# Sinkhorn-sorted attention and a mixture of experts: seven products for all four experts of the middle chunk, PSUM banks that stay in their pools, and loads in another order

## The chip, the cores and the metric

The kernel runs on one core of a Trainium2 chip. The metric is the device time of one execution in microseconds (us). Each kernel is executed several times and the median is given. The core has five engines that run beside one another: TensorE multiplies matrices, VectorE (DVE in the profile) and ScalarE (ACT) work on tiles in on-chip memory and evacuate the results of matmuls from PSUM, GpSimd (POOL) does some elementwise work and issues loads, and SyncE (SP) issues most other transfers. PSUM, where TensorE writes, has eight banks of 512 fp32 numbers per partition, and this kernel uses all of them.

## The reference, cut to what matters

```python
P = sort_net                                  # (4, 8, 8, 8)
for _ in range(5):                            # rows and columns normalised
    P = np.exp(P - P.max(-1)); P /= P.sum(-1); P /= P.sum(-2)
k_sorted = einsum('bhij,bhjcd->bhicd', P, k_blocks)    # blocks of 96 tokens mixed
v_sorted = einsum('bhij,bhjcd->bhicd', P, v_blocks)
attn = softmax(q_block @ k_sorted_block.T / 8)         # within each block
x = (attn @ v_sorted_block)  ->  (3072, 512)           # 4 batches x 768 tokens, 8 heads x 64
p = domain_probs / domain_probs.sum(-1)
out = sum over 4 experts e of  p[:, e] * (relu(x @ w1[e]) @ w2[e])   # 512 -> 1024 -> 512
```

Attention takes a small part of the matmul work, the four experts nearly all of it.

## The kernel before: the parts that the change touches

The tokens of each batch are worked through in three chunks of 256. A chunk has a first layer (x times w1, relu, times p, result in Hb) and a second layer (Hb times w2, result stored). While the experts of one batch are computed, the attention of a later batch is computed beside them: a plan names, for each slot between groups of matmuls, which stage is to run there. `st_v` mixes values, `st_k` keys, `st_q` transposes queries by DMA, `st_s` makes scores, `st_a` multiplies with the values, and `st_x` transposes the result into xT.

```python
PLANS = { ...                                           # (chunk, slot, stage, batch, part)
    1: [ ...
        (1, 3, st_k, 3, 1), (1, 4, st_v, 3, 2), (1, 4, st_q, 3, 3), (1, 4, st_bk, 3, 1), (1, 5, st_s, 3, 1),
        (1, 6, st_k, 3, 2), (1, 7, st_k, 3, 3), (1, 8, st_v, 3, 3), (1, 9, st_a, 3, 0), (1, 10, st_s, 3, 2),
        (1, 11, st_a, 3, 1), (1, 11, st_x, 3, 0), (1, 12, st_s, 3, 3), (1, 13, st_a, 3, 2), (1, 13, st_x, 3, 1),
        (1, 14, st_a, 3, 3), (2, 0, st_x, 3, 2), (2, 1, st_x, 3, 3),
    ], }
```

From the third chunk of batch 1 on (g = G0 = 5 of 12), a block of the first layer is computed after Winograd's scheme: instead of eight products of half-size blocks there are seven, and sums of the weights (s1, s3, n2, s4) and of the tokens (t1, n2, t3, t4) are formed beforehand. `seven` holds the seven products of one expert. X, Z and Q are PSUM banks; X must be a copy of Z at one point, and ScalarE makes it.

```python
def seven(g, e):
    ...
    def product(dst, lhs, rhs, first=False):            # eight matmuls of 128 columns
    ...
    def p1(): product(Z, "a11", "b11", True); nc.scalar.copy(X, Z)
    def p5(): product(Q, "s1", "t1", True)
    def p6(): product(X, "n2", "n2"); nc.scalar.copy(u2, X)
    def p2(): product(Z, "a12", "b21"); finish(0, 0, Z)
    def p7(): product(X, "s3", "t3"); nc.scalar.copy(u3, X); tt(t22, Q, u3, ALU.add)
    def p4(): product(X, "a22", "t4"); finish(1, 0, X)
    def p3(): product(Q, "s4", "b22"); tt(t12, Q, u2, ALU.add)
```

Before that chunk the banks belong to two pools, psM and psA, of two tiles of two banks each. At the chunk they are closed one after the other and given anew. The chunk's expert 0 is still computed directly (`chunk_first`), as banks of psM are free before those of psA:

```python
def last_banks(n):
    (openA, openM)[n].close()
    pool = ctx.enter_context(tc.tile_pool(name=f"ps7_{n}", bufs=1, space=PSUM, ...))
    ...
    nc.tensor.matmul(last["X"][n][:], w1sb[0][:, 0, 0:P], w1sb[0][:, 1, 0:512], start=True, stop=True)   # marks X as written

def last_chunk(g, slot=None):
    ...
    if lead:                                            # g == G0
        chunk_first(b, c, [0], 0, slot)                 # expert 0: 2 groups of 16 matmuls of 256 columns
        last_banks(0)
        last_tmp(g)
        prs = {1: seven(g, 1)}
        prs[1][1](); prs[1][5](); seven(g, 2)[5](); prs[1][2](); prs[1][6]()
        input_sums(0, 0, True); input_sums(0, 1, True)
        last_banks(1)
    else: ...                                           # later chunks: expert 0 was begun in the chunk before
    ...
    product(bankQ, sm(0), "t1");         nc.scalar.copy(p5[:], bankQ)
    product(bankA, sm(1), "t2", False);  nc.scalar.copy(u2[:], bankA)
    ...
    product(bankQ, blk(1, 0), "b22", False, range(2))   # experts 0 and 1
    ...
    product(bankA, blk(0, 1), "t3", False)
    ...
    tt(ob2, bankA, p5[:], ALU.add); tt(ob1, bankA, ob1, ALU.add)
    nc.sync.dma_start(o[:, 2 * c + 1, :], ob[:])
    ...
    product(bankQ, blk(1, 0), "b22", False, range(2, E), ...)   # experts 2 and 3
    tt(oa2, bankQ, u2[:], ALU.add)
    if final:
        nc.sync.dma_start(o[:, 2 * c, DH:Dm], oa2)
```

While the experts work on batch 0, GpSimd issues the loads of batch 1, all in one queue behind those of the experts' weights:

```python
for qd in range(2):
    for nm in ("v", "k"):
        load_natural(1, nm, qd)          # values, keys: four heads each
    if qd == 0:
        load_queries(1, range(2))        # queries of heads 0 and 1, in pieces of 64 numbers
```

Of the kernel before, what the change touches and what calls it, by code (L numbers as in the profile page):

```python
# [17 lines left out]
def kernel(  # L18
# [38 lines left out]

    openM, openA = [ctx.enter_context(ExitStack()) for _ in range(2)]
    psM = openM.enter_context(tc.tile_pool(name="psM", bufs=2, space=bass.MemoryType.PSUM))
    psA = openA.enter_context(tc.tile_pool(name="psA", bufs=2, space=bass.MemoryType.PSUM, side="right"))  # L60
    att = ctx.enter_context(tc.tile_pool(name="att", bufs=2))
# [368 lines left out]
    def st_a(b, pr):  # L430
        if b == B - 1 and pr >= H // 2 - 2:
            xsl = Sflat[:, ds((pr + 4) * NB * 2 * D, NB * 2 * D)].rearrange("p (i h d) -> p i h d", i=NB, h=2)[0:BLK]
        else:
            xsl = att.tile([P, NB, 2, D], F16, name=f"xsl_{b}_{pr}", tag="xsl")[0:BLK]
        xsls[(b, pr)] = xsl
        vs = vss[(b, pr // 2)]
        for hh in range(2):
            ET = ETs[2 * (pr % 2) + hh]
            ps = psa([P, 2, 512], F32, f"ps_a_{b}_{pr}_{hh}")
            for i in range(NB):  # L440
                nc.tensor.matmul(  # L441
                    ps[:, i // HB, ds((i % HB) * VW, D + 1)],
                    ET[:, ds(i * BLK, P)],
                    vs[:, i, 2 * (pr % 2) + hh, 0:D + 1],
                    start=True, stop=True,
                )
            normalize(ps, xsl, hh)
# [153 lines left out]
    def st_bk(b, qd):  # L601
# [25 lines left out]
            (1, 0, st_k, 3, 0), (1, 1, st_v, 3, 1), (1, 1, st_x, 2, 3), (1, 1, st_q, 3, 2), (1, 2, st_s, 3, 0),  # L627
            (1, 3, st_k, 3, 1), (1, 4, st_v, 3, 2), (1, 4, st_q, 3, 3), (1, 4, st_bk, 3, 1), (1, 5, st_s, 3, 1),
            (1, 6, st_k, 3, 2), (1, 7, st_k, 3, 3), (1, 8, st_v, 3, 3), (1, 9, st_a, 3, 0), (1, 10, st_s, 3, 2),
            (1, 11, st_a, 3, 1), (1, 11, st_x, 3, 0), (1, 12, st_s, 3, 3), (1, 13, st_a, 3, 2), (1, 13, st_x, 3, 1),  # L630
            (1, 14, st_a, 3, 3), (2, 0, st_x, 3, 2), (2, 1, st_x, 3, 3),
        ],
# [152 lines left out]
    def chunk(b, c, slot, done=()):  # L785
# [34 lines left out]

        if b or c:
            two = [psm([P, 2, 512], F32, f"ps_p{n}_{b}_{c}") for n in range(2)]
            bankA, bankB, bankC, bankQ = [two[n // 2][:, n % 2, 0:DH] for n in range(4)]
        if b:
            times(bankA, blk(0, 0), "b11", es)
            slot()
            times(bankB, blk(1, 0), "b21", es)
            slot()
            nc.scalar.copy(p1[:], bankA)
            tt(oa1, bankB, p1[:], ALU.add)  # L830
            times(bankQ, sm(0), "t1", es)
            nc.scalar.copy(p5[:], bankQ)
            slot()
            for e in es:
                h_sums(e, 3, True)
            times(bankA, sm(1), "t2", es, False)
            nc.scalar.copy(u2[:], bankA)
            slot()
            for e in es:
                h_sums(e, 4, True)  # L840
            times(bankC, blk(1, 1), "n4", es)
            nc.scalar.copy(ob1, bankC)
            slot()
            times(bankA, blk(0, 1), "t3", es, False)
            tt(ob2, bankA, p5[:], ALU.add)
            tt(ob1, bankA, ob1, ALU.add)
            store(1, ob)
            slot()
            times(bankQ, blk(1, 0), "b22", es, False)
            tt(oa2, bankQ, u2[:], ALU.add)  # L850
            slot()
            store(0, oa)
            return
# [94 lines left out]

    A_ORDER = (12, 13, 3, 6, 7, 8, 0, 1, 2, 9, 10, 11)
    As = []  # L950
# [41 lines left out]

    last = {}

    def last_banks(n):

        (openA, openM)[n].close()
        pool = ctx.enter_context(tc.tile_pool(name=f"ps7_{n}", bufs=1, space=bass.MemoryType.PSUM, side=("right", "left")[n]))
        for nm, m in (("X", 1), ("Z", 1), ("Q", 2)):
            last[nm] = last.get(nm, []) + [  # L1000
                pool.tile([P, 512], F32, tag=f"{nm}{i}", name=f"ps_{nm}{n}{i}") for i in range(m)
            ]

        nc.tensor.matmul(last["X"][n][:], w1sb[0][:, 0, 0:P], w1sb[0][:, 1, 0:512], start=True, stop=True)

    def last_tmp(g):

        room = []
        if g > G0:
            t = moe.tile([P, NKC, NB, BLK], F16, name="tmp7", tag="xT").rearrange("p k i x -> p (k i x)").bitcast(F32)  # L1010
            room += [t[:, ds(n * 512, 512)] for n in range(3)]
        for m in range(2):
            t = att.tile([P, NB, 4, VW], F16, name=f"tmp7_{g}_{m}", tag="vs").rearrange("p i h w -> p (i h w)")
            t = t[:, 0:2048].bitcast(F32)
            room += [t[:, 0:512], t[:, 512:1024]]
        for m in range(1 if g > G0 else 2):
            t = att.tile([P, NB, 2, D], F16, name=f"tmp7x_{g}_{m}", tag="xsl").rearrange("p i h d -> p (i h d)")
            room.append(t.bitcast(F32))
# [3 lines left out]
        else:  # L1022
            last["u2"] = last["t12"] = room[0::2]
            last["u3"] = last["t22"] = room[1::2]

    def seven(g, e):

        a, t, pb = As[e], Bs[g], pbs[divmod(g, R // 2)]
        n = e - (g == G0)
        X, Z = [last[nm][n % len(last[nm])][:] for nm in ("X", "Z")]  # L1030
        u2, u3, t22, t12 = [last[nm][n % len(last[nm])] for nm in ("u2", "u3", "t22", "t12")]
        Q = last["Q"][e if n == e else (0, 0, 1, 3)[e]][:]
        tt = nc.vector.tensor_tensor
# [21 lines left out]

        def p1():
            product(Z, "a11", "b11", True)
            nc.scalar.copy(X, Z)  # L1058

# [29 lines left out]
    def last_begin(g):  # L1089
        last["e0"] = seven(g, 0)  # L1090
        last["e0"][1]()
        last["e0"][5]()

    def last_chunk(g, slot=None):
        b, c = divmod(g, R // 2)
        final = g == GN - 1
        lead = int(g == G0)
        if lead:
            chunk_first(b, c, [0], 0, slot)
            last_banks(0)  # L1100
            last_tmp(g)
            prs = {1: seven(g, 1)}
            prs[1][1]()
            prs[1][5]()
            seven(g, 2)[5]()
            prs[1][2]()
            prs[1][6]()
            input_sums(0, 0, True)
            input_sums(0, 1, True)
            last_banks(1)  # L1110
        else:
            last["e0"][2]()
            prs = {0: last["e0"]}
        for e in range(1 + lead, E):
            prs[e] = seven(g, e)
        for e in range(1 + lead, E):
            now, prev = prs[e], prs[e - 1]
            now[1]()
            prev[7]()
            if e > 1 + lead:  # L1120
                prs[e - 2][12]()
            if not lead or e > 2:
                now[5]()
            now[2]()
# [10 lines left out]

        def product(ps, lhs, rhs, first=True, es=range(E), between=None, at=E - 1):
            for e in es:
                if e == at and between:
                    between()
                for f in range(KH):  # L1140
                    nc.tensor.matmul(  # L1141
                        ps, lhs(e, f), Ts[e][rhs][:, f, :],
                        start=(first and e == 0 and f == 0), stop=(e == E - 1 and f == KH - 1), skip_group_check=True,
# [26 lines left out]
        for e in range(E):  # L1170
            h_sums(e, 4, True)
        if lead:
            for e in range(E):
                h_sums(e, 3, True)
            input_sums(0, 2, True)
        product(bankQ, sm(0), "t1")
        nc.scalar.copy(p5[:], bankQ)
        product(bankA, sm(1), "t2", False)
        nc.scalar.copy(u2[:], bankA)
        if not lead:  # L1180
            for e in range(E):
                h_sums(e, 3, True)
        product(bankQ, blk(1, 0), "b22", False, range(2))
        if not final:
# [8 lines left out]
        nc.sync.dma_start(o[:, 2 * c + 1, :], ob[:])  # L1193
        if lead:
            input_sums(0, 3, True)
        product(bankQ, blk(1, 0), "b22", False, range(2, E), None if final else last["e0"][6], 3)
        tt(oa2, bankQ, u2[:], ALU.add)
        if final:
            nc.sync.dma_start(o[:, 2 * c, DH:Dm], oa2)
        else:  # L1200
            nc.sync.dma_start(o[:, 2 * c, :], oa[:])


    PLAN_A = [
        (1, 8, 1, 0, True), (1, 8, 1, 1, True), (1, 8, 1, 2, True), (1, 10, 1, 3, True),
        (1, 8, 2, 0), (1, 8, 2, 1), (1, 9, 3, 0), (1, 10, 3, 1), (1, 11, 2, 2), (1, 12, 3, 2), (1, 13, 2, 3),
        (2, 0, 3, 3),
    ]
# [94 lines left out]
    h_q(0, 1, vec)  # L1303
    second_layer0(0, next_stages)
    for qd in range(2):
        for nm in ("v", "k"):
            load_natural(1, nm, qd)
        if qd == 0:
            load_queries(1, range(2))
    chunk_first(0, 0, [1, 2], 1, next_stages)  # L1310
# [64 lines left out]
```

The softmax here doesn't subtract the row's maximum and nothing guards it: scores larger than these inputs give would overflow.

## Time and profile before

| | before |
|---|---|
| time, median of three executions | 363.17 us (362.46 to 363.51) |
| span in the profile | 362.4 us, granted TensorE clock 1.00 throughout |
| VectorE, ScalarE, GpSimd busy | 276.8, 173.6, 134.1 us |
| DMA queues, share of 16 engines | 41.6% GpSimd's queue, 27.4% SyncE's |
| HBM read, written | 42.00 MB, 6.34 MB |

A line of the waits names who waited, for whom, and gives microseconds in total, the number of waits and the longest. A line of the chain gives the start, the length and the engine with its tile. A line in order of time gives the start, the length, the engine, the line of the kernel, the operation, the tiles and the number of instructions merged in it; in square brackets stands the idle time ahead of it and what ended it. Starts are exact; the ends of matmuls are modelled and include the way through the array.

### The profile page before, as it was taken

The page shows a single profiled execution, that of the slowest core. Times are in us where ns is not written, and L with a number is a line of the kernel's source. Part 1 is how long each engine was busy: PE and PEld are TensorE (multiplying, and loading weights), DVE is VectorE, ACT ScalarE, POOL GpSimd, SP SyncE. Part 2 cuts the span into 40 slices and gives each one's busy share as a digit, 9 for nine tenths or more (in the row PEclk, how much of TensorE's full clock was granted, in tenths as well). Part 3 has the DMA queues.
Part 4 walks back from the last instruction along what each step waited for, and adds up shares of the span by engine and source line. Part 5 has one row for each costly group of instructions (what it writes and reads, how often), then busy time and mean ns, then how long its engine had stood idle before and what let it go on. Part 6 is the DMA issues. An engine that isn't in the chain of part 4 may idle for free.

```text
span 362.4 us, 10776 instructions
## 1 busy us (share of the span) xinstructions
PE 354.0 (98%) x4589; PEld 315.0 (87%) x4589; DVE 276.8 (76%) x560; ACT 173.6 (48%) x305; POOL 134.1 (37%) x148
## 2 busy tenths in 40 slices
PE   8899999989999999999999999999999999999996
PEld 8785857778888888988889999999999998999995
DVE  5654898769788777868978978867779679587794
ACT  2664330451434355377938257165283481561740
POOL 8872010736022330000626318137055082180470
PEclk9999999999999999999999999999999999999999
DMA  7999999999999999935995210210401201102101
GB/s 99 207 207 231 209 209 202 194 187 194 214 116 142 203 127 173 165 70 69 179 192 88 60 60 2 60 60 3 89 32 50 70 3 58 62 2 63 56 15 46
DMA packets 71676, 40.47 MB, mean 112 GB/s; under 512 B 40518, under 2 KB 66380, under 8 KB 71628
## 3 DMA queue, kind: packets, MB, share of 16 engines
q0 software_dynamic: 36560, 19.93, 41.6%
q1 hardware_dynamic: 35068, 19.85, 27.4%
q8 instruction: 36, 0.59, 0.7%
q14 instruction: 12, 0.10, 0.1%
HBM read 42.00 MB, written 6.34 MB: 133 GB/s over the span
## 4 chain that ended last, share of the span: by engine, by line
PE 75%; DMA 18%; DVE 3%; SPq 1%; ACT 1%; issue 1%; POOL 0%; DVEq 0%; ACTq 0%; POOLq 0%
PE ps_Q L1141 24%; PE ps_h L768 13%; PE ps_p L753 10%; PE ps_X L1038 10%; DMA arena<-in_q_dram 8%; PE ps_Q L1038 7%; PE ps_Z L1038 7%; DMA w<-in_moe_w_dram 6%; DMA vs<-arena 2%; DMA qT<-arena 2%; PE ps_a L441 2%; PE ps_s L406 1%; SPq L368 1%; PE ps_v L354 1%; PE ps_k L387 1%
## 5 line engine op out<-in xcount | busy, mean ns | idle before, releaser
L1051 POOL TENSOR_TENSOR Hb<-tmp,pb 128x512 f16<-128x512 f32 x40 | 50.8, 1277 | 84.3 <-ACT tmp L1050 83.1
L768 PE MATMUL ps_h<-xT,w 128*128 128x256 f16 x576 | 67.8, 273 | 0.0
L768 PEld LDWEIGHTS <-w 128*128 128x128 f16 x576 | 55.1, 98 | 7.4
L774 DVE SCALAR_TENSOR_TENSOR Hb<-ps_h,pb 128x1024 f16<-128x1024 f32 x36 | 44.0, 1223 | 19.8 <-PE ps_h L768 19.6
L1141 PEld LDWEIGHTS <-Hb 128*128 128x128 f16 x560 | 53.4, 98 | 5.6
L1038 PEld LDWEIGHTS <-w 128*128 128x128 f16 x864 | 52.4, 98 | 1.0
L1141 PE MATMUL ps_Q<-w,Hb 128*128 128x256 f16 x336 | 43.4, 273 | 0.0
L1038 PEld LDWEIGHTS <-arena 128*128 128x128 f16 x552 | 33.4, 98 | 0.3 <-issue 0.2
L413 ACT ACTIVATE ET<-ps_s 96x768 f16<-96x768 f32 x24 | 18.1, 802 | 28.4 <-PE ps_s L406 28.1
L121 POOL DMA_DIRECT2D arena<-in_q_dram x24 | 19.9, 836 | 26.9 <-DMA qT<-arena 16.6
L1038 PE MATMUL ps_X<-kT,arena 128*128 128x128 f16 x384 | 29.3, 219 | 0.1
L1074 DVE TENSOR_TENSOR tmp<-ps_Q,tmp 128x512 f32<-128x512 f32 x26 | 18.0, 692 | 14.6 <-ACT tmp L1073 10.4
L1058 ACT COPY ps_X<-ps_Z 128x512 f32<-128x512 f32 x27 | 15.4, 570 | 28.3 <-PE ps_Z L1038 27.9
L396 ACT CAST kT<-ps_k 64x384 f16<-64x384 f32 x48 | 22.7, 473 | 12.8 <-PE ps_k L387 11.8
L739 DVE TENSOR_TENSOR Sb<-Hb 128x512 f16<-128x512 f16 x45 | 26.3, 609 | 0.9 <-POOL Hb L1051 0.8
L1141 PE MATMUL ps_Q<-T,Hb 128*128 128x256 f16 x224 | 26.7, 273 | 0.0
L1050 ACT ACTIVATE tmp<-tmp 128x512 f32<-128x512 f32 x40 | 25.4, 634 | 1.2 <-DVE tmp L1074 1.0
L753 PEld LDWEIGHTS <-Hb 128*128 128x128 f16 x232 | 21.9, 98 | 3.0
L1141 PEld LDWEIGHTS <-Sb 128*128 128x128 f16 x224 | 21.9, 98 | 2.5
L1065 ACT COPY tmp<-ps_X 128x512 f32<-128x512 f32 x26 | 15.2, 586 | 13.2 <-PE ps_X L1038 13.2
L1051 POOL TENSOR_TENSOR Hb<-tmp7x,pb 128x512 f16<-128x512 f32 x14 | 19.0, 1356 | 5.7 <-ACT tmp7x L1050 5.7
L1044 DVE SCALAR_TENSOR_TENSOR Hb<-ps_X,pb 128x512 f16<-128x512 f32 x27 | 18.5, 684 | 2.7 <-PE ps_X L1038 2.7
(205 smaller groups left out, 652.7 us busy)
## 6 DMA issues: line engine op xcount, KB each, us to landing
w<-in_moe_w_dram POOLq DMA_DIRECT2D x7, 1024.0 KB, 27.4
pb<-p_dram SPq DMA_DIRECT2D x12, 512.0 KB, 5.4
arena<-in_k_dram POOLq DMA_DIRECT2D x8, 384.0 KB, 8.8
arena<-in_v_dram POOLq DMA_DIRECT2D x8, 384.0 KB, 8.9
vs<-arena SPq DMA_DIRECT2D x36, 66.0 KB, 5.7
arena<-in_q_dram POOLq DMA_DIRECT2D x24, 96.0 KB, 7.3
out_dram<-ob SPq DMA_DIRECT2D x9, 256.0 KB, 2.0
out_dram<-oa SPq DMA_DIRECT2D x8, 256.0 KB, 2.3
```

Source lines behind the costliest of these rows:

```text
L121: nc.gpsimd.dma_start(t[:, h // 2, :, h % 2, :], q[b, h].rearrange("(t p) d -> p t d", p=P))
L396: nc.scalar.copy(kT[ds(D * hh, D), r], pk[ds(D * r, D), hh].rearrange("p a (i c) -> p a i c", c=CP),)
L413: nc.scalar.activation(ETs[2 * (pr % 2) + hh][:, 0:S].rearrange("c (a x) -> c a x", a=2), pss[hh][0:BLK, :, 0:HS], AF.Exp, bias=0.0, scale ...
L739: tt(sm[0], blk(0, 1), blk(1, 1), ALU.add)
L753: nc.tensor.matmul(ps, lhs(e, f), Ts[e][rhs][:, f, :], start=(first and e == es[0] and f == 0), stop=(done and e == es[-1] and f == KH - 1 ...
L768: nc.tensor.matmul(ps[:, f, :], w1sb[e][:, kc, ds((4 * g + f) * P, P)], xT[:, kc, ds(2 * c * P, 2 * P)], start=(kc == 0), stop=(kc == NKC ...
L774: nc.vector.scalar_tensor_tensor(out=Hb[:, e, ds(4 * g, 4), :], in0=ps[:], scalar=0.0, op0=ALU.max, in1=pb[:, ds(e, 1), :].broadcast_to([P ...
L1038: nc.tensor.matmul(dst[:, ds(f * P, P)], a[lhs][:, k, ds(f * P, P)], t[rhs][:, k, :], start=(first and f == 0 and k == 0), stop=(f == KH - ...
L1044: nc.vector.scalar_tensor_tensor(out=Hb[:, e, ds(i * KH, KH), ds(j * P, P)], in0=src.rearrange("p (f x) -> p f x", f=KH), scalar=0.0, op0= ...
L1050: nc.scalar.activation(src, src, AF.Relu, bias=0.0, scale=1.0)
L1051: nc.gpsimd.tensor_tensor(Hb[:, e, ds(i * KH, KH), ds(j * P, P)], src.rearrange("p (f x) -> p f x", f=KH), pb[:, ds(e, 1), ds(j * P, P)].b ...
L1141: nc.tensor.matmul(ps, lhs(e, f), Ts[e][rhs][:, f, :], start=(first and e == 0 and f == 0), stop=(e == E - 1 and f == KH - 1), skip_group_ ...
```

## The change: what it does and what it is for

1. The third chunk of batch 1 computes expert 0 by seven products too. It is begun in the chunk before, within that chunk's last product, as the later chunks do it for one another.
2. For this the eight banks stay in the two pools for the whole kernel. The chunk before takes X, Z and two Q banks from psM as ordinary tiles and uses them for its own sums as well; the third chunk takes the other four from psA.
3. The input sums of expert 0 (s1, s3, n2, s4) are formed earlier, on VectorE, in slots of the second chunk; their place in memory moves (A_ORDER), and so does that of two attention tiles (xsl), which now lie where the values of batch 3 lay. So these values must be used up sooner: `st_v(3, 3)` moves from slot 8 to slot 4.
4. The queries of heads 0 and 1 of batch 1 are loaded ahead of the values and keys.
5. At the very end the last column half of the output is computed and stored in two pieces of 128 columns, in two banks and through two queues.

```diff
-    openM, openA = [ctx.enter_context(ExitStack()) for _ in range(2)]
-    psM = openM.enter_context(tc.tile_pool(name="psM", bufs=2, space=bass.MemoryType.PSUM))
-    psA = openA.enter_context(tc.tile_pool(name="psA", bufs=2, space=bass.MemoryType.PSUM, side="right"))
+    psM = ctx.enter_context(tc.tile_pool(name="psM", bufs=2, space=bass.MemoryType.PSUM))
+    psA = ctx.enter_context(tc.tile_pool(name="psA", bufs=2, space=bass.MemoryType.PSUM, side="right"))
...
-            xsl = Sflat[:, ds((pr + 4) * NB * 2 * D, NB * 2 * D)]...
+            xsl = arena[:, ds((pr + 2) * NB * 2 * D, NB * 2 * D)]...
...
-            (1, 3, st_k, 3, 1), (1, 4, st_v, 3, 2), (1, 4, st_q, 3, 3), (1, 4, st_bk, 3, 1), (1, 5, st_s, 3, 1),
-            (1, 6, st_k, 3, 2), (1, 7, st_k, 3, 3), (1, 8, st_v, 3, 3), (1, 9, st_a, 3, 0), (1, 10, st_s, 3, 2),
+            (1, 3, st_k, 3, 1), (1, 4, st_q, 3, 3), (1, 4, st_v, 3, 2), (1, 4, st_v, 3, 3), (1, 4, st_bk, 3, 1), (1, 5, st_s, 3, 1),
+            (1, 6, st_k, 3, 2), (1, 7, st_k, 3, 3), (1, 9, st_a, 3, 0), (1, 10, st_s, 3, 2),
...
-            (1, 14, st_a, 3, 3), (2, 0, st_x, 3, 2), (2, 1, st_x, 3, 3),
+            (2, 0, st_x, 3, 2), (2, 1, st_x, 3, 3),
...                                   # in chunk(), the chunk before
-        if b or c:
+        if (b, c) == divmod(G0 - 1, R // 2):
+            last_banks(1)
+            bankA, bankB, bankC, bankQ = [last[nm][at][:, 0:DH] for nm, at in (("X", 1), ("Z", 1), ("Q", 2), ("Q", 3))]
+        elif b or c:
...
-            times(bankQ, blk(1, 0), "b22", es, False)
+            if last["X"]:
+                last_tmp(G0, range(1), ())
+                last_begin(G0)
+
+                def between():
+                    last["e0"][6]()
+                    st_a(B - 1, H // 2 - 1)
+
+                times(bankQ, blk(1, 0), "b22", es, False, True, between, 2)
+            else:
+                times(bankQ, blk(1, 0), "b22", es, False)
...
-    A_ORDER = (12, 13, 3, 6, 7, 8, 0, 1, 2, 9, 10, 11)
+    A_ORDER = (12, 13, 14, 6, 7, 8, 0, 1, 2, 9, 10, 11)
...
+        pair = [(psa, psm)[n]([P, 2, 512], F32, f"ps7_{n}_{m}") for m in range(2)]
+        for nm, at, m in (("X", n, 0), ("Z", n, 1), ("Q", 2 * n, 2), ("Q", 2 * n + 1, 3)):
+            last[nm][at] = pair[m // 2][:, m % 2]
...
     def last_begin(g):
-        last["e0"] = seven(g, 0)
-        last["e0"][1]()
-        last["e0"][5]()
+        last["e0"] = e0 = seven(g, 0)
+        if g == G0:
+            e0[1](lambda: (e0[5](), written(1)))      # written: the marking matmul; p1 copies Z to X after it
+        else:
+            e0[1]()
+            e0[5]()
...                                   # in last_chunk()
+        last["e0"][2]()
         if lead:
-            chunk_first(b, c, [0], 0, slot)
+            last["e0"][7]()
+            slot()
             last_banks(0)
...
+        ends = [(bankQ, ds(0, P), nc.scalar), (bankB, ds(P, P), nc.sync)] if final else [(bankQ, ds(0, DH), nc.sync)]
+        for bank, part, _ in ends:
+            product(bank[:, part], sm(0), "t1", part=part)
+            nc.scalar.copy(p5[:, part], bank[:, part])
...
+        early = 1 if final else 2
+        for bank, part, _ in ends:
+            product(bank[:, part], blk(1, 0), "b22", False, range(early), part=part)
...
+        for bank, part, queue in ends:
+            product(bank[:, part], blk(1, 0), "b22", False, range(early, E), ..., 3, part)
+            tt(oa2[:, part], bank[:, part], u2[:, part], ALU.add)
+            if final:
+                queue.dma_start(o[:, 2 * c, DH:Dm][:, part], oa2[:, part])
...
     PLAN_A = [
+        (1, 1, 0, 0, True), (1, 3, 0, 1, True), (1, 5, 0, 2, True), (2, 0, 0, 3, True),
...
-        (2, 0, 3, 3),
+        (1, 14, 3, 3),
...
+    load_queries(1, range(2))
     for qd in range(2):
         for nm in ("v", "k"):
             load_natural(1, nm, qd)
-        if qd == 0:
-            load_queries(1, range(2))
```

## The prediction

> **What bounds the kernel.** I read the page's first part, then the waits of TensorE, then the chain backwards from the longest of them, then TensorE in order of time around the chunk that is changed, then the end.
>
> ```profile
> PE 354.0 (98%) x4589; PEld 315.0 (87%) x4589; DVE 276.8 (76%) x560; ACT 173.6 (48%) x305; POOL 134.1 (37%) x148
> ...
> PE ps_s L406 <- DMA qT<-arena: 1.9, 1, 1.9
> PE ps_R L305 <- DVE sn L293: 1.1, 1, 1.1
> PE ps_w L249 <- DVE Hb L148: 1.1, 1, 1.1
> ```
>
> TensorE is busy for 354.0 of 362.4 us at full clock. Only two things can move the time: fewer or smaller matmuls, and TensorE's idle time, 8.4 us in all. Of that, 3.4 us lie behind the last matmul, some 2.2 us at the start (the two waits of 1.1), and one wait stands in the middle: 1.9 us on a transposed query tile. The chain shows where it comes from, and GpSimd in order of time shows the loads in their queue:
>
> ```profile
> 40.44 27.25 DMA arena<-in_q_dram
> 67.75 6.01 DMA qT<-arena
> 73.89 0.52 PE ps_s L406 x16
> ...
> 27.66 0.81 POOL L110 DMA_DIRECT2D arena<-in_v_dram  x1 [0.66 <-PE ps_mv L483]
> 28.46 0.75 POOL L110 DMA_DIRECT2D arena<-in_k_dram  x1
> 34.70 0.82 POOL L121 DMA_DIRECT2D arena<-in_q_dram  x1 [5.48 <-DMA w<-in_moe_w_dram]
> 40.44 0.82 POOL L121 DMA_DIRECT2D arena<-in_q_dram  x1 [4.92 <-DMA w<-in_moe_w_dram]
> ```
>
> The second query head of batch 1 was issued at 40.44 and landed at 67.7, behind the weights and the first quarters of values and keys. SyncE could have transposed from 61.5 (its load of pb was issued at 61.13) and waited until 67.75; the transpose landed at 73.8, and the scores, ready on TensorE at 72.0, began at 73.89.
>
> Then the chunk itself, TensorE in order of time:
>
> ```profile
> 181.82 1.91 PE L753 MATMUL ps_p<-w,Hb 128*128 128x256 f16 x16
> 183.56 0.94 PE L441 MATMUL ps_a<-vs,ET 96*128 96x65 f16 x16
> 184.34 3.66 PE L768 MATMUL ps_h<-xT,w 128*128 128x256 f16 x32
> 187.83 0.38 PE L1004 MATMUL ps_X<-w 128*128 128x512 f16 x1
> 188.05 0.61 PE L1038 MATMUL ps_Z<-xT,w 128*128 128x128 f16 x8
> ```
>
> Durations here include the pipe's tail; the starts are what counts. 32 matmuls of 256 columns take 187.83 - 184.34 = 3.49 us (109 ns each); a product of eight matmuls of 128 columns takes 0.447 us (starts 193.18, 193.62, 194.07), 55.9 ns each. The 16 matmuls of ps_a take 0.48 us elsewhere but 0.78 here: the second half waits for a psA tile. And the end:
>
> ```profile
> 357.93 1.04 PE L1141 MATMUL ps_Q<-w,Hb 128*128 128x256 f16 x8
> 358.97 0.33 SPq L1193 DMA_DIRECT2D out_dram<-ob  x1
> 359.07 0.42 DVE L1197 TENSOR_TENSOR oa<-ps_Q,u 128x256 f32<-128x256 f32 x1
> 359.53 0.33 SPq L1199 DMA_DIRECT2D out_dram<-oa  x1
> ```
>
> The 256 KB of ob and the 128 KB of oa are issued within 0.56 us; their packets run as one stream from 359.7 to 360.9 at 330 to 380 GB/s.
>
> [...] order of issue is order of landing (62.6, 64.6, 65.2, 67.7). [...]
>
> **The change, part by part.** *Queries first.* Nothing is added; two loads pass two others. The landings in the trace give about 2.0 us for a quarter of values or keys and 3.1 us for the pair of query heads (67.7 - 64.6; their packets are under 512 B, and run between 62 and 65 us). In the new order the pair should land near 67.7 - 4.0 = 63.7 or a little sooner, the values near 65.5, the keys near 67.7. SyncE can then issue the transpose about 4 us earlier. It stands in one ring behind pb, whose packets now run from 65.0 to 69.5; so the tile lands between 70 and 72.8, against 72.0 when TensorE wants it: I take 0.3 us as what is left of the wait. The values are wanted at 65.18 (first ps_v) and the keys at 68.45: another 0.2 us at risk. Net: 1.9 - 0.5 = 1.4 us.
>
> *Expert 0 of the third chunk by seven products.* Between the end of the t3 product (181.5) and the b11 product of the chunk (197.28) lie 15.78 us. Matmul time in it, from the starts: b22 1.75, two ps_a 0.96, the direct layer 3.49, 19 products 8.49, two marking matmuls 0.44, sum 15.13; so 0.65 us are gaps, 0.30 at the ps_a tile, the rest after the marking matmuls, where ScalarE copies Z to X with too little work beside it. After: b22 1.75, ps_a 0.96, 26 products 11.62, marks 0.44, sum 14.77: 0.36 less. Gaps: p1, p5 and the mark now lie between the two ps_a stages, so the tile is free (that stage's evacuation ended 2.5 us after t3, the second half begins at 3.2); the half of b22 (0.87 us) covers the copy of Z. From the end of t3 as zero, TensorE then stands at 0.48 (ps_a), 0.93 and 1.38 (p1, p5), 1.60 (mark), 2.47 (b22), 2.92 (p6), 3.40 (ps_a), 4.27 (b22), 4.72 and 5.17 (p2, p7), 5.39 (mark), 6.29 (p1, p5 of expert 1). ScalarE copies expert 0's u3 from 5.3 to 5.9 and expert 1's Z from 5.9 to 6.45, so p2 starts at 6.5: a wait of 0.2. p6 ends at 7.4. VectorE has two normalisations (3.3 to 5.0), an addition, a finish, t22 and s4 before the fourth token sum, which is done near 7.5: p4 waits 0.1. After that each expert takes seven products as in the later chunks, which show no wait. Gaps 0.3; gain 0.36 + 0.35 = 0.7 us.
>
> *Input sums of expert 0* move to VectorE between 156 and 166 us, 0.6 us each. Its idle stretches there are 0.85, 0.52 and 0.75 us, with two psM tiles ahead of it: no cost. *The last value stage* moves from 170.0 to about 161.9 us with its two matmuls and one cast; same work, no cost on TensorE. Banks taken from the running pools rather than from a closed one cost nothing by themselves: the same readers must be done.
>
> *The end.* 32 matmuls of 128 replace 16 of 256 twice: 32 x 55.9 against 16 x 109 is 0.04 us more each. With E the end of the last matmul's stream (358.8), before: VectorE starts at E + 0.27, takes 0.42, the last packet at E + 2.1. After: ob's addition runs 0.44 us earlier relative to E, as three experts instead of two are left; its 256 KB are gone by about E + 1.0. The last addition has 128 columns, about 0.28 us (0.69 for 512, 0.42 for 256); its 64 KB are issued at E + 0.6 and, after the 0.7 us seen between issue and packet, are gone by E + 1.5. Gain about 0.55, less 0.08: 0.5 us.
>
> Sum: 1.4 + 0.7 + 0.5 = 2.6 us off 363.17, or 360.6 us.
>
> **The rivals.** *The query wait only changes its name.* The transpose may still follow pb and the 256-byte loads of the next heads, and land near 73; or the values, now third, land late and hold the first ps_v. For it: 0.1 us of slack for the values, and pb took 8.4 us to land in this stretch. Against: before, transpose packets began only near 70, when pb was nearly through. Then 0.3 us of gain are left and the time is 361.7. *The new lead is bound by VectorE and ScalarE.* In the 15.78 us VectorE is busy for 13.05; seven products bring two more finishes and two additions (2.6 us start to start) and s4, and take away two evacuations of 1.2 and two input sums. If TensorE waits at each expert, 0.5 us are lost and the time is 361.3 to 361.8. *Everything hidden works, and the wait for queries was the only slack* that some later load needed: a load bound by the queue would show up again as a wait near 90 to 125 us; the transfers there start from TensorE's own progress, so I give it little.
>
> **Range and chances.** Head 0.3 to 1.9, lead 0.2 to 0.9, end 0.2 to 0.6; not all at one edge, and half a microsecond for the spread of the runs (362.46 to 363.51): 359.7 to 362.2. Two per cent would be 7.3 us, more than all the idle time that can be reached; losing as much would need a new wait that nothing shows. Faster by over 2%: 0.01; within: 0.98; slower: 0.01.
>
> **What would show it.** Right: no or hardly a wait of ps_s on qT; the transpose issued near 63.5; the stretch from t3 to b11 near 15.1 us; the last store's data ending 1.5 us after the last matmul. Wrong: ps_v waiting on the load of values; TensorE idle at the fourth token sum or at the copies; a new wait on a vs or xT transfer in batch 2.

## The result and the profile after

The changed kernel takes 445.97 us (445.40 to 449.34, median of six executions); beside it, on the same chip, the kernel before takes 363.03 us (362.46 to 363.51). The ratio is 1.230 (95% interval 1.226 to 1.234). Predicted were 360.6 us, with a range of 359.7 to 362.2.

The page of the changed kernel, first the busy times, then the clock that TensorE was granted in 40 slices:

```profile
PE 387.5 (87%) x4645; PEld 337.7 (75%) x4645; DVE 277.0 (62%) x563; ACT 176.8 (40%) x311; POOL 136.0 (30%) x150
...
PEclk9999999999999999989979998899698799999799
```

The other engines do what they did before (VectorE 277.0 us against 276.8), so no work has been added there. TensorE is idle for 447.6 - 387.5 = 60.1 us instead of 8.4, and its own work takes 33.5 us longer, although it has about the same number of matmuls (4645 against 4589, with more of the small ones). From slice 18 on (190 to 201 us, in the third chunk of batch 1, soon after the seven products begin) the clock is no longer always full: 0.946 in the mean of the whole span.

The waits of TensorE after (who waited, for whom: us in total, number, longest):

```profile
PE ps L1048 <- DVE Hb L1054: 24.5, 36, 1.2
PE ps L1048 <- DVE tmp L1086: 19.2, 13, 1.6
PE ps L1048 <- ACT tmp L1077: 1.8, 6, 0.3
PE ps L1147 <- DVE tmp L1086: 1.5, 1, 1.5
...
PE ps_a L440 <- DMA vs<-arena: 0.6, 1, 0.6
PE ps_s L405 <- DMA qT<-arena: 0.4, 1, 0.4
```

Before, no wait of these products is listed. Now the products (line 1048) wait 36 times for `finish` (line 1054, relu of X or Z into Hb) and 13 times for the addition that makes t22 (line 1086, reads Q). There is a second thing to read here: the tile is called `ps`, where before it was ps_X, ps_Z or ps_Q. X, Z and the two Q are no longer tiles of their own.

The second chunk of batch 2 in order of time shows which product waits for which reader. TensorE (start, length, line, operation, number; in brackets the idle time ahead and what ended it):

```profile
260.87 1.05 PE L1048 MATMUL ps<-xT,w 128*128 128x128 f16 x16 [0.29 <-ACT tmp L1077]
262.32 0.61 PE L1048 MATMUL ps<-kT,Sb 128*128 128x128 f16 x8 [0.39 <-DVE Hb L1054]
264.32 0.61 PE L1048 MATMUL ps<-kT,arena 128*128 128x128 f16 x8 [1.40 <-DVE tmp L1086]
264.77 0.61 PE L1048 MATMUL ps<-xT,w 128*128 128x128 f16 x8
266.16 0.84 PE L1048 MATMUL ps<-kT,arena 128*128 128x128 f16 x8 [0.78 <-DVE Hb L1054]
...
276.66 1.01 PE L1048 MATMUL ps<-kT,arena 128*128 128x128 f16 x8 [1.55 <-DVE tmp L1086]
277.47 1.06 PE L1048 MATMUL ps<-xT,w 128*128 128x128 f16 x8
279.31 1.01 PE L1048 MATMUL ps<-kT,arena 128*128 128x128 f16 x8 [0.78 <-DVE Hb L1054]
280.12 1.06 PE L1048 MATMUL ps<-ET,w 128*128 128x128 f16 x8
280.97 1.06 PE L1048 MATMUL ps<-xT,w 128*128 128x128 f16 x8
```

and VectorE in the same stretch:

```profile
263.58 0.69 DVE L1086 TENSOR_TENSOR tmp<-ps,tmp 128x512 f32<-128x512 f32 x1 [1.31 <-ACT tmp L1085]
265.41 0.69 DVE L1054 SCALAR_TENSOR_TENSOR Hb<-ps,pb 128x512 f16<-128x512 f32 x1 [1.14 <-PE ps L1048]
```

The product at 264.32 is p5 of expert 1. It writes that expert's Q, which nobody is reading. It starts 0.05 us after VectorE has finished the addition at 263.58 (ends at 264.27), and that addition reads the Q of expert 0: the other half of the same two-bank tile. The product at 266.16 is p6 of expert 1. It writes X of this expert, and starts 0.06 us after `finish` at 265.41 has read Z of the same pair (ends at 266.10). So TensorE, which used to work in one bank while VectorE and ScalarE emptied its neighbour, now takes turns with them. VectorE in its turn waits for ScalarE and TensorE (1.31 and 1.14 us in the brackets): each hand-over puts one engine's time behind the other's.

The last lines of the TensorE fence show the second loss. The product of eight matmuls at 280.12 is followed by the next at 280.97: 0.85 us, or 106 ns for a matmul of 128 columns, against 55.9 ns before. The granted clock of this stretch (280 to 281 us) is 0.50.

### The profile page after: what moved, and what is told of

The parts are those of the page before. It is cut to its first block, busy times and chain, and to the rows that moved or that the text cites. A ratio compares the mean times of both kernels' runs of the same rounds, so it can differ in the third digit from the quotient of the medians.

```text
span 447.6 us, 10915 instructions
## 1 busy us (share of the span) xinstructions
PE 387.5 (87%) x4645; PEld 337.7 (75%) x4645; DVE 277.0 (62%) x563; ACT 176.8 (40%) x311; POOL 136.0 (30%) x150
## 4 chain that ended last, share of the span: by engine, by line
PE 67%; DVE 13%; DMA 9%; ACT 5%; issue 3%; SPq 1%; POOL 1%; DVEq 0%; ACTq 0%; POOLq 0%
PE ps L1048 21%; PE ps L1147 17%; PE ps_h L767 12%; PE ps_p L752 6%; DVE Hb L1054 5%; DMA w<-in_moe_w_dram 3%; DVE tmp L1086 3%; DMA qT<-arena 2%; ACT tmp L1085 2%; PE ps_o L695 2%; PE ps_h L660 2%; DVE Sb L738 2%; DMA vs<-arena 2%; PE ps L752 1%; DMA room<-arena 1%
## 5 line engine op out<-in xcount | busy, mean ns | idle before, releaser
L1048 PE MATMUL ps<-kT,arena 128*128 128x128 f16 x504 | 44.7, 244 | 37.4 <-DVE tmp L1086 19.2
L1054 DVE SCALAR_TENSOR_TENSOR Hb<-ps,pb 128x512 f16<-128x512 f32 x56 | 38.6, 690 | 56.8 <-PE ps L1048 56.7
L1048 PEld LDWEIGHTS <-w 128*128 128x128 f16 x896 | 66.1, 110 | 9.1 <-issue 7.9
L767 PEld LDWEIGHTS <-w 128*128 128x128 f16 x544 | 52.0, 98 | 7.0
L1147 PE MATMUL ps<-w,Hb 128*128 128x256 f16 (+1 forms) x352 | 45.3, 274 | 2.5 <-DVE tmp L1086 1.5
L1077 ACT COPY tmp<-ps 128x512 f32<-128x512 f32 x27 | 15.8, 586 | 61.1 <-PE ps L1048 61.1
L1086 DVE TENSOR_TENSOR tmp<-ps,tmp 128x512 f32<-128x512 f32 x27 | 18.7, 691 | 30.5 <-ACT tmp L1085 29.3
L1048 PE MATMUL ps<-xT,w 128*128 128x128 f16 x384 | 33.3, 240 | 3.6 <-DVE Hb L1054 1.7
L1070 ACT COPY ps<-ps 128x512 f32<-128x512 f32 x28 | 16.0, 570 | 39.7 <-PE ps L1048 39.1
L1147 PE MATMUL ps<-T,Hb 128*128 128x256 f16 x224 | 26.7, 273 | 0.5 <-DVE oa L1168 0.5
L1048 PE MATMUL ps<-room,w 128*128 128x128 f16 x288 | 25.0, 241 | 1.9 <-DVE Hb L1054 1.0
```

The costliest lines, as they stand in the source:

```text
L767: nc.tensor.matmul(ps[:, f, :], w1sb[e][:, kc, ds((4 * g + f) * P, P)], xT[:, kc, ds(2 * c * P, 2 * P)], start=(kc == 0), stop=(kc == NKC ...
L1048: nc.tensor.matmul(dst[:, ds(f * P, P)], a[lhs][:, k, ds(f * P, P)], t[rhs][:, k, :], start=(first and f == 0 and k == 0), stop=(f == KH - ...
L1054: nc.vector.scalar_tensor_tensor(out=Hb[:, e, ds(i * KH, KH), ds(j * P, P)], in0=src.rearrange("p (f x) -> p f x", f=KH), scalar=0.0, op0= ...
L1147: nc.tensor.matmul(ps, lhs(e, f), Ts[e][rhs][:, f, part], start=(first and e == 0 and f == 0), stop=(e == E - 1 and f == KH - 1), skip_gro ...
```

## The experiments

Three theories stood after the traces. **A**: the change put X with Z, and each two Q, into one tile of two banks, and a writer waits for the readers of the whole tile. **B**: the lowered clock is the first cause, and the waits follow from slow matmuls. **C**: the new start of the third chunk and the moved sums and stages brought VectorE out of step with TensorE.

### Four banks as four tiles

Everything of the change is kept, except that X, Z and the Q are tiles of one bank. For this the running pools must again be closed one after the other.

```diff
-        pair = [(psa, psm)[n]([P, 2, 512], F32, ...) for m in range(2)]
-        last["X"][n], last["Z"][n] = pair[0][:, 0], pair[0][:, 1]        # and Q, Q from pair[1]
+        (openA, openM)[n].close()
+        pool = ctx.enter_context(tc.tile_pool(name=f"ps7_{n}", bufs=1, space=PSUM, ...))
+        last["X"][n] = pool.tile([P, 512], F32, tag="XZ0", ...)           # Z and two Q likewise
```

> The changed kernel with one thing undone: X, Z and the two Q banks of each half are four tiles of one bank again, from a pool opened in place of the closed one; every other part of the change stays. Theory A (two banks in one tile make TensorE wait for VectorE and ScalarE reading the other bank[...]): all of the 83 us goes, mean clock 1.00, no waits of the products on finishes or t22, and the rest of the change shows: 360.0 to 362.5 us. Theory B (the extra products or the earlier start of the third chunk bring TensorE under a lower granted clock, and the waits follow from that): stays above 430 us. Theory C (the half of batch 3's stages that were moved, or the sums on VectorE, delay everything after): stays above 400 us.

Measured: 364.23 us, ratio to the kernel before 0.999 (0.996 to 1.003), clock 1.00. Its busy times and the longest waits of its TensorE:

```profile
PE 352.8 (97%) x4645; PEld 314.6 (87%) x4645; DVE 278.5 (77%) x563; ACT 176.3 (48%) x311; POOL 136.6 (38%) x150
...
PE ps_R L305 <- DVE sn L293: 2.0, 1, 2.0
PE ps_o L696 <- DMA w<-in_moe_w_dram: 1.1, 1, 1.1
PE ps_w L249 <- DVE Hb L148: 1.1, 1, 1.1
PE ps_X L753 <- DVE Hb L774: 1.0, 1, 1.0
```

None of the waits of the products is left but one of 0.2 us. The loss of 83 us is gone with the tiles, while the new start of the chunk, the moved sums, the moved value stage, the loads and the split end are all still there. C falls. What doesn't appear is a gain; this is taken up below, as is the new wait of ps_X, which comes from closing the pool.

### The kernel before, with nothing but the shared tiles

```diff
-        for nm, m in (("X", 1), ("Z", 1), ("Q", 2)):
-            last[nm] = ... pool.tile([P, 512], F32, ...)
+        pair = [pool.tile([P, 2, 512], F32, tag=f"pair{m}", ...) for m in range(2)]
+        for nm, m in (("X", 0), ("Z", 1), ("Q", 2), ("Q", 3)):
+            last[nm] = last.get(nm, []) + [pair[m // 2][:, m % 2]]
```

> The kernel before with one thing done: X and Z are the two halves of one tile of two banks, and so are the two Q; pools are closed and opened as before, and no other part of the change is in it. Theory A: 435 to 450 us, granted clock below 0.97, the same waits as in the changed kernel. Theories B and C: 363 us.

Measured: 438.67 us, ratio 1.206 (1.198 to 1.213), clock 0.96. Waits of its TensorE:

```profile
PE ps_pair L1037 <- DVE Hb L1043: 24.2, 34, 1.4
PE ps_pair L1037 <- DVE tmp L1073: 17.7, 12, 1.6
```

The same two waits at the same two places, in nearly the same numbers, in a kernel that has nothing else of the change. Together with the run before this settles A: the tiles alone bring the loss, and without them it does not come. The kernel before asks for its four banks in the same order, X, Z, Q, Q, so X has Z beside it in both kernels. What differs is only which banks make one tile, and the waits go by that.

### One pair at a time

Both are the version with own banks, with one of the pairs put back into one tile: first the two Q, then X and Z.

```diff
+        pair = pool.tile([P, 2, 512], F32, tag="QQ", ...)
+        last["Q"][2 * n], last["Q"][2 * n + 1] = pair[:, 0], pair[:, 1]      # first run
...
+        pair = pool.tile([P, 2, 512], F32, tag="XZ", ...)
+        last["X"][n], last["Z"][n] = pair[:, 0], pair[:, 1]                  # second run
```

> The changed kernel with X and Z in tiles of their own and the two Q of each half in one tile. Theory A, each shared tile costs by its own waits: the waits of the fifth products on t22 remain (about 3 us in each of seven chunks by the trace), those on finishes go: 380 to 410 us. If only one kind of pair matters, 361 or above 430 us.

> The changed kernel with X and Z in one tile and each Q in a tile of its own. Theory A: the waits on finishes remain (about 3.7 us in each of seven chunks), those on t22 go: 385 to 420 us. [...]

Measured: Q shared 394.90 us, ratio 1.085 (1.078 to 1.093); X and Z shared 406.39 us, ratio 1.117 (1.109 to 1.125). The waits of TensorE, first with Q shared, then with X and Z shared:

```profile
PE ps_QQ L1053 <- DVE tmp L1091: 19.7, 13, 1.8
PE ps_QQ L1152 <- DVE Sb L741: 2.3, 5, 0.5
```

```profile
PE ps_XZ L1053 <- DVE Hb L1059: 32.8, 42, 1.3
PE ps_XZ L1053 <- ACT tmp L1082: 1.8, 6, 0.3
```

Each pair brings its own wait, and only its own. The clock is 1.00 in both profiles, so B falls too: TensorE waits at full clock. The sizes also say how much of the loss is the clock. Against the kernel before on its own chip, Q costs 30.6 us, X and Z 42.1 us, and own banks 0.4; the sum of the two increments is 30.2 + 41.7 = 71.9 us. Both together, in the changed kernel, cost 82.9 - 0.4 = 82.5. The rest of 10.6 us goes with the half clock, which shows only where both pairs are shared.

The profiled spans say the same in another way. From own banks to the changed kernel the span grows by 83.9 us (the profiled execution of the changed kernel is its slowest, 449.34 us). The two single pairs add 24.1 and 31.7 us of idle time and 5.0 and 8.5 us of busy time. That busy time is no work: a product of eight matmuls takes 0.61 us in the records, whose ends are modelled, and 0.447 from start to start, and behind every wait the 0.16 us between the two are no longer overlapped; for the 27 waits that Q brings and the 49 of X and Z this makes 4.3 and 7.8 us. In the changed kernel the idle time grows by 49.2 us, which is 6.6 less than the sum, and the busy time by 34.7, which is 21.2 more. The granted clock of this trace is 0.50 for 48 us in all. A matmul of 128 columns took 106 ns there instead of 55.9, so about half of the 48 us is lost, 24 us, which is near the 21.2.

In the changed kernel the granted clock falls to 0.50 nine times before the last matmul, for 3.4 to 6.8 us at a time and 48 us in all; else it is 1.00. In the 3.4 us ahead of these nine falls TensorE is idle for 53 to 62% of the time, against 20% in the mean from 186 to 443.86 us. The fence of the second chunk of batch 2 shows one such place: from 262.98 to 266.38 us, where the clock falls, TensorE works for 1.28 of 3.40 us, and a wait of each pair falls into it, 1.40 us for the addition that makes t22 and 0.78 for `finish`. With one pair shared only one of the two waits is there; those of Q reach 1.8 us, longer than any wait of the products in the changed kernel (1.6), and the mean clock is 1.000. So in these runs the lowered clock did not go with the longest single wait. That the share of idle time brings it down is not shown; no run changed that alone.

### Where the expected 2.6 us stayed: the parts one by one

With own banks the three wanted parts could be looked at. Two runs take one of them out of the version with own banks: the old order of the loads, then the old end.

```diff
-    load_queries(1, range(2))           # and back behind the first values and keys
...
-        ends = [(bankQ, ds(0, P), nc.scalar), (bankB, ds(P, P), nc.sync)] if final else [...]
+        ends = [(bankQ, ds(0, DH), nc.sync)]
```

> The kernel with banks of their own, and the loads of queries again behind the first values and keys. If the query wait was removed by the order of the loads and the gain kept, this is 1.0 to 1.9 us slower than the kernel with banks of their own; if the gain is given back later to another transfer, within 0.4 us of it.

> The kernel with banks of their own, and the last column half again in one piece with one store. If the split end is worth what was worked out, 0.5 us slower than with the split[...].

Measured: with the old loads 363.84 us, ratio 0.999 (0.995 to 1.002), with the old end 364.44 us, ratio 1.000 (0.997 to 1.004). The profile of the first was taken in a disturbed execution and isn't read. Neither differs from 364.23.

The kernel before with the new loads and the new end, without the change of the third chunk:

```diff
+    load_queries(1, range(2))           # ahead of values and keys
...
+        ends = [(bankQ, ds(0, P), nc.scalar), (bankB, ds(P, P), nc.sync)] if final else [...]
```

> The kernel before with the queries first and the split end, without the new third chunk. The distance to the kernel with banks of their own is what seven products for expert 0 bring: 0.7 us slower than it by the prediction, 0 or faster if the new lead is bound by VectorE and ScalarE. Against the kernel before: 1.5 to 2.4 us faster.

Measured: 363.88 us, ratio 0.998 (0.995 to 1.002). And the opposite, own banks and the new third chunk alone, both taken back as in the first diff of this section (the Q banks are placed first, as in the next run):

> The kernel with the Q banks first, with the old order of loads and the old end: what is left of the change is seven products for expert 0 of the third chunk. By the traces this stretch is 0.76 us shorter than before: 0.4 to 0.9 us faster than the kernel before, with the query wait of 1.9 us back, or of up to 0.5 us less if the start is later on this chip.

Measured: 364.19 us, ratio 1.001 (0.999 to 1.004). So none of the three is worth anything that the times can show; their intervals are some 0.3%, or 1 us, to either side. The traces tell why, part by part.

**The third chunk.** From the start of t3, the last product but one of the chunk before, to the first matmul of b11, with which the second layer of the chunk begins, are 197.28 - 179.57 = 17.71 us before and 197.32 - 180.39 = 16.93 in the last run: the predicted gain is there (0.78 us, 0.7 predicted), and so is the predicted wait of 0.2 on the copy of Z. But ahead of it stands the wait that closing a pool brings. TensorE with the new chunk alone:

```profile
168.11 0.50 PE L387 MATMUL ps_k<-arena 128*128 128x128 f16 x6
169.59 1.91 PE L753 MATMUL ps_X<-w,Hb 128*128 128x256 f16 x16 [0.98 <-DVE Hb L774]
...
188.82 0.61 PE L1052 MATMUL ps_Z<-xT,w 128*128 128x128 f16 x8 [0.21 <-ACT ps_X L1074]
```

The product at 169.59 is the first in the banks of the closed pool. TensorE could have begun at 168.44 (the six matmuls of ps_k take 0.33 us in the kernel before, 167.93 to 168.26); it waited 0.98 us, and with the part of the pipe no longer overlapped lost 1.14, for VectorE's evacuation of the last first-layer group. In the kernel before, the same product has no wait:

```profile
167.93 0.50 PE L387 MATMUL ps_k<-arena 128*128 128x128 f16 x6
168.26 1.91 PE L753 MATMUL ps_p<-w,Hb 128*128 128x256 f16 x16
```

It goes into the pool's next tile, whose readers were done one group earlier. The changed kernel, which closes no pool, has no wait there either (168.36, behind ps_k at 168.03).

Is it the place of the banks, or the closing? The four single banks are placed in another order, so that X does not lie where the last group lay:

```diff
-        X, Z, Q, Q = pool.tile(...), ...        # order of allocation
+        Q, Q, X, Z = pool.tile(...), ...
```

> The kernel with banks of their own, and the four single banks given in the order Q, Q, X, Z instead of X, Z, Q, Q. In the first order the first product of the chunk before waits 1.0 us for VectorE's last evacuation of the first layer. If that is because X lies in the banks of the last first-layer tile, the wait goes here (Q is wanted 3.5 us later) and this is 0.6 to 1.0 us faster: 0.990 to 0.998 of the kernel before. If closing a pool waits for all of its readers, the 1.0 us stays.

Measured: 364.58 us, ratio 1.002 (1.000 to 1.005), and the same line in the waits:

```profile
PE ps_X L753 <- DVE Hb L774: 1.0, 1, 1.0
```

So it is the closing: the first tile of the new pool waits for the last reader of the old one, in either order of the banks. The 0.98 us and their drain are more than the 0.78 that the new start of the chunk gains.

Can other work be put there? In the next run the key stage before the last group and the attention stage of two slots later run in that place too, 0.33 + 0.49 = 0.82 us of matmuls beside the stage that stood there. (It builds on a version described below, in which the queries are transposed earlier.)

```diff
-            (1, 6, st_k, 3, 2), (1, 7, st_k, 3, 3), (1, 9, st_a, 3, 0), ...
+            (1, 7, st_k, 3, 2), (1, 7, st_k, 3, 3), (1, 7, st_a, 3, 0), ...
```

> This is the version with own banks, all three wanted parts and the queries transposed ahead of pb; now the key stage of slot 6 and the attention stage of slot 9 run in slot 7, between the last first-layer group and the first product in the banks of the closed pool. TensorE waited 0.98 us there for VectorE's last evacuation. If closing the pool costs only that wait, 1.0 us of other work (two key stages and one ps_a, 0.45 + 0.45 + 0.49 us) fills it: the wait is under 0.2 us, the stretch from the last ps_h group to the end of the chunk is about 0.9 us shorter, span near 361.1, time near 362.9, ratio 0.997 to 0.998. If the closing has another cost behind it (the next product waits, or the stages wait for a psA tile), the wait appears at ps_a or ps_k and the ratio stays at 1.000.

Measured: 365.95 us, ratio 1.007 (1.005 to 1.010). The waits of TensorE:

```profile
PE ps_a L441 <- ACT kT L396: 1.7, 1, 1.7
PE ps_R L305 <- DVE sn L293: 1.4, 1, 1.4
PE ps_w L249 <- DVE Hb L148: 1.1, 1, 1.1
PE ps_a L441 <- DVE xsl L423: 1.0, 1, 1.0
```

The wait for the closed pool is gone, and 2.7 us have come in its place. The three stages in a row need four tiles of psA, which has two: the attention stage waits for ScalarE to empty the tile of the keys, and its second half for VectorE, which is still busy with the last group and must normalise the first half. The gap behind this evacuation was no free place for stages that need evacuations themselves. What the new start of the chunk gains could not be had in any version run here.

**The head.** SyncE after, in order of time, and the chain of the changed kernel in the same place:

```profile
61.68 0.38 SPq L212 DMA_DIRECT2D pb<-p_dram  x1
62.16 2.18 SPq L374 DMA_TRANSPOSE qT<-arena  x1
```

```profile
62.16 10.65 DMA qT<-arena
72.81 0.14 issue
72.95 0.52 PE ps_s L405 x16
```

The queries landed early enough: the transpose was issued at 62.16, 5.6 us sooner than before. But it needed 10.65 us instead of 6.01, behind pb (the factors p of a chunk) in the same queue and beside the loads of values and keys. The scores began at 72.95 instead of 73.89, and about half of that was given back at 124.55, where ps_a waited 0.57 us for the mixed values (124.98 before). Their transfer (vs) is issued by SyncE behind the value stage; with the old order of the loads and the new chunk alone ps_a waits there too, 0.35 us, so the new order is not what brings this wait.

In the next run SyncE issues the transpose ahead of pb:

```diff
-            (0, 7, st_q, 1, 0), ...
+            (0, 5, st_q, 1, 0), ...
```

> As the kernel with the Q banks first, with the transpose of the first queries two slots sooner, so that it stands ahead of the load of pb in SyncE's ring. If its place behind pb is why the tile still lands at 73 us, it lands between 67 and 70 us here, the wait of the first scores is 0, and TensorE reaches them up to 0.4 us sooner; the whole changes by at most 0.5 us, as a later transfer takes it back. If the loads of the DMA engines as a whole set its landing, it lands after 71.5 us.

Measured: 363.80 us, ratio 1.000 (0.998 to 1.003). The transpose landed at 70.5 (61.67 + 8.8), between the two times that were named for it, and the scores begin at 72.78 with no wait on it. The last run makes the same edit in the kernel before with the new loads and the split end:

> The kernel before with the queries loaded first, transposed ahead of pb, and the split end; nothing of the third chunk is changed and no pool is closed earlier. Head 0.4 to 1.0 us, end 0.15 us: 0.6 to 1.1 us off, ratio 0.997 to 0.9985. If the start of the weights decides the head rather than the queries, the ratio stays at 1.000 and the scores begin no sooner than 73.5.

Measured: 363.57 us against 363.08 (362.25 to 365.00) of the kernel before beside it, ratio 1.000 (0.998 to 1.003). TensorE and SyncE in this run:

```profile
72.88 0.51 PE L406 MATMUL ps_s<-qT,kT 64*128 64x96 f16 x16
...
63.03 1.32 SPq L375 DMA_TRANSPOSE qT<-arena  x1
64.45 0.54 SPq L213 DMA_DIRECT2D pb<-p_dram  x1
```

The wait is wholly gone, and still the scores begin only 1.0 us sooner. The other 0.9 were lost ahead of it: the first matmul of the experts (ps_h) began at 19.34 in this execution and at 18.46 in the profile before. These starts differ from execution to execution (18.46 to 20.54 us in thirteen profiles), and so do the landings of the queries. Two more profiles have the old order of the loads. With the new chunk alone, TensorE was ready for the scores at 72.91 instead of 72.00 and SyncE could transpose at 66.09 instead of 67.75; the wait was 0.34 us, and the scores began at 73.25. In the kernel before with the shared tiles, whose head is that of the kernel before, SyncE could transpose at 65.35; nothing waited, and the scores began at 72.67. So the 1.89 us were the chance of one execution, an early TensorE and late queries. The scores begin at 72.67 to 73.89 with the old order (three profiles), at 72.32 to 74.12 with the new one (seven), and at 72.75 to 72.88 with the transpose ahead of pb as well (three). No gain of the new order can be read from these, and a smaller one would be hidden by the spread of the runs (2.75 us among those of the kernel before beside the last run).

**The end.** From the start of the product of T and Sb in the last chunk to the end of the span: 8.84 us before, 8.82 with own banks and the old end, 8.65 with own banks and the split end, 8.64 in the kernel before with the split end. The gain is 0.2 us. SyncE, ScalarE and VectorE at the end of the version with own banks:

```profile
360.20 0.33 SPq L1202 DMA_DIRECT2D out_dram<-ob  x1
...
360.43 0.37 ACTq L1209 DMA_DIRECT2D out_dram<-oa  x1
...
360.71 0.29 DVE L1207 TENSOR_TENSOR oa<-ps_Q,u 128x128 f32<-128x128 f32 x1 [0.31 <-PE ps_Q L1151]
...
361.03 0.33 SPq L1209 DMA_DIRECT2D out_dram<-oa  x1
```

The last addition takes 0.29 us and the last store is issued 0.83 us behind the store of ob, as planned; but the packets of all three stores run as one stream from 361.0, and the last comes at 362.3. In the changed kernel even this end has a wait of the shared tile: the second piece lies in bankB, the other half of the pair of bankA, and TensorE waits 0.23 us at 443.86 for the addition to ob that reads bankA.

The trace of the new chunk alone closes the sum. From the scores to the product of T and Sb in the last chunk it takes 280.62 us, 0.95 more than before: 0.30 at ps_a for the mixed values, 0.19 where two value stages now follow one another, 1.14 at the closed pool, -0.78 in the new chunk, -0.18 in small gaps between b11 and t3, and 0.27 in the last chunk (344.83 to 345.55 for a product that takes 0.45 before). The last of these stands in all six profiles that have the new chunk and banks of their own, and in none of the three that have neither the new chunk nor shared tiles. It goes back to ScalarE, which copies X to u2 at 344.91 instead of 344.60; TensorE's next product into X starts 0.05 us after that copy. Why the copy starts later is left open.

## Why the prediction was wrong, point by point

- **The step that failed** is the sentence "Banks taken from the running pools rather than from a closed one cost nothing by themselves: the same readers must be done." A pool of the running kind hands out tiles of two banks. So the banks became halves of a tile, and the readers of the neighbour must be done as well. The price was 74 us by itself (438.67 against 364.28 of the kernel before beside it). The change had the reason in plain sight, `pair[m // 2][:, m % 2]`; I asked who had used the bank before, and not who else uses its tile now. The changed kernel guards by pair of banks; with a tile for each bank (364.23 us) all these waits but one of 0.2 us were not there.
- **"Losing as much would need a new wait that nothing shows"**: the new waits are some 70, each short. No view of the kernel before could show them, but the order of the seven products could: p6 writes X right behind p2, whose Z VectorE is then reading, and p5 of experts 1 and 3 writes one Q while the addition for t22 reads the other.
- **The mark and the copy of Z to X** (predicted wait 0.2): right, 0.21.
- **The lead chunk**, 0.7: the mechanism was right and the size near (0.78). The step counted from 181.5, where the record of t3 ends with the pipe's tail; the next product starts at 181.33, so the gaps before were 0.82 us and not 0.65; after, they are 0.40 and not 0.3. What was missing from the sum in the versions without shared tiles is the 1.14 us that closing the pool one chunk earlier costs; the prediction had no such term, as the change does not close pools.
- **The queries**, 1.4: the loads moved as predicted (landed at 61.8, predicted 63.7), the transpose did not. The step had it land "between 70 and 72.8"; it landed at 72.8, as in the first rival, and 0.94 us were gained, of which about 0.5 went back at the mixed values. The term was also too large at its root: the wait of 1.89 us came from an early start and late queries in one execution, and in two others with the old order it was 0.34 us and nothing.
- **The end**, 0.5: 0.2. With E the end of the last matmul's stream, the step had the 256 KB of ob gone at E + 1.0 and the last packet at E + 1.5. With own banks E is 360.44 (the last addition starts 0.27 later); the packets of the three stores, the same 384 KB as before, run from E + 0.6 to E + 1.9. They take as long as before (1.3 us against 1.2) and only start sooner.
- **The rivals**: that VectorE and ScalarE bind the new start did not happen with own banks. That some later transfer takes back what the queries gain, which was given little, came in part: it is the wait of 0.57 us at 124.55. No rival named the tile.

## What to carry to other kernels

When banks are regrouped into larger tiles, list for each bank who reads its neighbours in the tile while it is being written: here the waits went by tile and cost 74 us by themselves, so banks that are to be written and read side by side should be tiles of their own. Closing a pool to get such tiles is not free either: here the first new tile waited 0.98 us for the last reader of the old pool. Put it where the readers are done. And a wait on a transfer in one profile is worth less than its length where the engine's own start and the landing of the data vary by as much. Look for the same wait in other executions before it is put into a sum.

## What was not expected of the hardware

- With both pairs shared, the waits were short, none over 1.6 us, and yet the granted clock of TensorE was 0.50 in nine stretches, 48 us in all, each behind 3.4 us in which TensorE had been idle for 53 to 62%. With one pair shared, with waits of up to 1.8 us, it was 1.000 in the mean. So two losses of 30.2 and 41.7 us made 82.5 together. Single executions of the kernel before have a mean slightly under 1.00 as well (0.99 in its slowest, 367.11 us).
- A wait of TensorE cost more than the trace puts in the bracket: about 0.16 us per wait (0.61 - 0.447) are no longer overlapped and, with the modelled ends, counted as busy. Of the 13.5 us by which the busy time grows in the two single-pair runs together, the waits explain 12.1 in this way.
- The transpose of the first query tile took 6.0 to 7.0 us where it was issued 3.5 to 6.6 us behind pb (three profiles), 8.6 to 8.8 ahead of pb (three), and 10.0 to 10.7 right behind pb (seven).
